# One region that keeps every engine's instructions in the order in which a planner emits them

## The chip, the cores and the metric

The kernel runs on one core of a Trainium2 chip. The metric is the device time of one launch in microseconds (us). The engines of a core run side by side, each through a list of instructions of its own: TensorE (PE, matrix products into PSUM banks), VectorE (DVE), ScalarE (ACT), GpSimd (POOL) and SyncE (SP, which here only starts DMA transfers). An engine takes its list in order, and an instruction that needs a result of another engine waits at the head of the list.

## The reference

Three layers, for 4 batches, 8 heads, 768 steps and 48 numbers per head (4 * 768 = 3072 rows of 8 * 48 = 384 numbers):

```python
f = 1.0 / (1.0 + np.exp(-f_logit))
for t in range(S):
    state = f[:, :, t, :, None] * state + np.einsum('bhd,bhe->bhde', k[:, :, t], v[:, :, t])
    y[:, :, t] = np.einsum('bhd,bhde->bhe', q[:, :, t], state)
...
xn = (x - mu) / np.sqrt(var + 1e-06) * g_ln
x = x + np.maximum(xn @ w_ch1, 0.0) @ w_ch2            # 384 -> 1536 -> 384
...
h = np.maximum(x @ w_in, 0.0)                          # 384 -> 1024
for k in range(K):
    conv_out += conv_w[k][None, None, :] * hp[:, k:k + S, :]
return h * (1.0 / (1.0 + np.exp(-conv_out))) @ w_out   # 1024 -> 384
```

## The kernel before

The sequence is cut into 24 chunks of 128 rows, and three chunks make a unit (8 units). Every chunk goes through gated attention, a LayerNorm and a first MLP (in the code `c1` and `c2`), and every unit through the second layer (`h2`, three taps along the rows, a gate, and the product `o` with the output weights).

**Attention.** DVE makes scans `e` (L471) and `w` (L473) of the forget gates, multiplies q and k by them (L477, L479, L481, L483), PE forms scores in the tile `sc__144` (L497), DVE masks them into `am` (L502), ACT and DVE split them in a high and a low half `as` (L316, L618). ACT also copies transposed keys `kts` out of PSUM, for the state update (PE L529).

**LayerNorm.** DVE L640 and L641 make mean and variance, POOL (L649) turns the variance into the factor `rs`, DVE L653 makes `xn`, and ACT and DVE (L657) split it into two halves `xs`, which a DMA transposes to `xnT`.

**Weights.** They arrive as 64-bit floats in three rotating buffers `raw` and are turned into 32-bit ones on DVE by three instructions, L374, L377 and L380, with the tile `tw` between them. `w__0` and `w__1` are the two buffers of the result. From there ACT and PE (L407, L408) or ACT and DVE (L421) make two half-precision parts.

**Second layer.** For each of the 8 slices of 128 columns PE makes `h2` (L795 to L797), ACT copies it with ReLU to `hr` and multiplies it by the middle tap into `cv`, DVE adds the other two taps (L812, L817). After two slices ACT takes the tanh, DVE multiplies (L827), ACT makes the high half of `g` and DVE the low half (L832). PE then makes `o` (L846 to L848), ACT copies it to the one buffer `ob`, and a DMA takes it out.

**What sets the order.** All this work is written down as jobs of the class `Plan`, each with an engine, a duration that the kernel assumes, a due time, the jobs it needs, and the buffers that it takes and frees. `Plan.run` lists them in Python: again and again it takes, among the jobs that could start next on their engine, the one that is due first, and emits its instructions.

```python
                first = min(c)[0]
                pick = min((k, t, z) for t, k, z in c if t <= first + 0.1)
...
            j = ready[e].pop(z)
            ...
            j.fn()
            j.at = t
            free[e] = t + j.dur
```

So the emission order is the planner's. Before the change it isn't the order on the engines: the framework has a scheduler of its own, which takes the emitted instructions and picks an order for each engine again. The few instructions behind `P.run()` judge whether the inputs lie in the range for which this path is exact (the tile `vr`, one small product on PE at L942); a general path behind a branch is not taken.

Of the kernel before, what the change touches and what calls it, by code (L numbers as in the profile page):

```python
# [205 lines left out]
def fast_path(  # L206
# [7 lines left out]
    P = Plan()  # L214
# [695 lines left out]
    for i, w_ in enumerate((w1s, w2s, wis, wos)):  # L910
        h_ = w_[:, 0].rearrange("p a b -> p (a b)")
        n = h_.shape[1] // 6
        for z in range(6):
            norm2(lambda h_=h_, z=z, n=n: h_[:, z * n:(z + 1) * n], n, 1.0, nrm[:, i, z:z + 1],
                  500.0 + z, [J["late"]])
    P.run()

    n = NACC + NT + NT * NP
    cmp_ = const.tile([128, n], F32, name="cmp")
# [211 lines left out]
@with_exitstack  # L1131
def tile_gated_linear_attention__then__ln_mlp__then__conv_glu(
    ctx: ExitStack, tc: tile.TileContext, q, k, f, v, vd, qk_, f_, gln, w1, w2, wi, cw, wo, out
):
    nc = tc.nc
    vpool = ctx.enter_context(tc.tile_pool(name="verdict", bufs=1))
    bad = vpool.tile([1, 1], I32, name="bad")
    fast_path(tc, v, qk_, f_, gln, w1, w2, wi, cw, wo, out, bad)
    r = nc.values_load(bad, min_val=0, max_val=1)
    with tc.If(r > 0):  # L1140
        pairs = [a.rearrange("b (p j) d s -> (b p) j d s", j=2) for a in (q, k, f, vd)]
        general_path(tc, *pairs, gln, w1, w2, wi, cw, wo, out)
# [44 lines left out]
```

## Time and profile before

| | |
|---|---|
| time, median of 3 runs | 644.81 us (642.97 to 645.51) |
| time of the profiled execution | 643.46 us |
| its span, first to last instruction | 641.4 us |
| busy PE / DVE / ACT / POOL | 586.1 / 501.0 / 386.2 / 42.1 us |
| busy share of the span | 91% / 78% / 60% / 7% |
| chain that ended last | PE 53%, DVE 27%, ACT 8%, DMA 4%, issue 4%, POOL 2% |

The time of the profiled execution is 2.06 us more than its span; that part lies outside the instructions. The busy shares are means over stages that differ, and the chain that ended last tells which engine the end of the kernel went through.

### The profile page before, as it was taken

Reading aid. Unit: us, or ns where it says so; the run is one execution under the profiler, and the core shown is the slowest. Engines: PE = TensorE matmul, PEld = TensorE weight load, DVE = VectorE, ACT = ScalarE, POOL = GpSimd, SP = SyncE. Lnnn points to the kernel's source line nnn. Section 1 sums busy time; section 2 is a strip of 40 time slices with the busy share of each in tenths; the row PEclk is TensorE's granted clock in tenths of the full one; section 3 lists DMA queues with packets and bytes.
Section 4 is the critical chain, followed back from the end, with each engine's and each line's share of the span. In section 5 each row is a group of like instructions: output and inputs, shape, how many; then the busy total and the mean of one; then the engine's idle time right before and its main releaser. Section 6 shows DMA issues by size and latency. Waiting matters only on the chain.

```text
span 641.4 us, 11836 instructions
## 1 busy us (share of the span) xinstructions
PE 586.1 (91%) x4680; PEld 392.7 (61%) x4680; DVE 501.0 (78%) x801; ACT 386.2 (60%) x798; POOL 42.1 (7%) x102
## 2 busy tenths in 40 slices
PE   1869898999798999999989999999989999999993
PEld 1758586767465666666656666666646666665551
DVE  6999989999999898976898787787895773326681
ACT  5888767779896575643675573554563662316471
POOL 3010110010101100010001000010000000000000
PEclk9979999999979899999989999999989999999998
DMA  8757567623224212541521203433221002001001
GB/s 255 184 168 186 175 141 181 189 55 75 68 58 123 63 41 48 143 77 28 103 54 54 80 20 75 118 78 58 46 42 50 14 13 51 25 1 38 25 13 42
DMA packets 75262, 52.24 MB, mean 81 GB/s; under 512 B 51904, under 2 KB 67264, under 8 KB 75200
## 3 DMA queue, kind: packets, MB, share of 16 engines
q1 hardware_dynamic: 75200, 51.42, 31.9%
q8 instruction: 38, 0.62, 0.4%
q14 instruction: 24, 0.20, 0.1%
HBM read 34.63 MB, written 4.72 MB: 61 GB/s over the span
## 4 chain that ended last, share of the span: by engine, by line
PE 53%; DVE 27%; ACT 8%; DMA 4%; issue 4%; POOL 2%; SPq 0%; DVEq 0%; ACTq 0%
PE B L675 5%; PE B L676 5%; PE B L677 5%; PE B L744 5%; PE B L746 5%; PE B L745 5%; PE B L848 4%; PE B L846 4%; PE B L847 4%; PE B L795 2%; PE B L796 2%; PE B L797 2%; DVE tw L377 2%; DVE cv L812 2%; DVE cv L827 2%
## 5 line engine op out<-in xcount | busy, mean ns | idle before, releaser
L675 PE MATMUL B<-xnT,w1s 128*128 128x128 f16 (+1 forms) x432 | 109.2, 275 | 3.0 <-DMA xnT<-xs 3.0
L677 PE MATMUL B<-xnT,w1s 128*128 128x128 f16 (+1 forms) x432 | 109.0, 275 | 0.3 <-ACT w1s L316 0.3
L676 PE MATMUL B<-xnT,w1s 128*128 128x128 f16 (+1 forms) x432 | 109.2, 275 | 0.0
L744 PE MATMUL B<-w2s,hh 128*128 128x384 f16 x288 | 94.5, 329 | 3.1 <-ACT w2s L316 2.1
L746 PE MATMUL B<-w2s,hh 128*128 128x384 f16 x288 | 94.7, 329 | 1.0 <-DVE hh L681 1.0
L745 PE MATMUL B<-w2s,hh 128*128 128x384 f16 x288 | 94.7, 329 | 0.9 <-DVE w2s L421 0.7
L681 DVE SCALAR_TENSOR_TENSOR hh<-B,hh 128x384 f16<-128x384 f32 (+1 forms) x90 | 51.4, 578 | 35.5 <-ACT hh L316 35.1
L795 PE MATMUL B<-x2T,wis 128*128 128x385 f16 x192 | 64.0, 334 | 5.9 <-ACT hr L316 5.9
L846 PE MATMUL B<-wos,g 128*128 128x384 f16 x192 | 63.7, 332 | 3.6 <-ACT g L316 3.6
L848 PE MATMUL B<-wos,g 128*128 128x384 f16 x192 | 63.3, 331 | 2.5 <-DVE g L832 2.4
L796 PE MATMUL B<-x2T,wis 128*128 128x385 f16 x192 | 64.1, 334 | 0.0
L797 PE MATMUL B<-x2T,wis 128*128 128x385 f16 x192 | 64.1, 334 | 0.0
L316 ACT ACTIVATE hh<-B 128x384 f16<-128x384 f32 (+1 forms) x90 | 44.5, 504 | 32.2 <-PE B L677 32.0
L847 PE MATMUL B<-wos,g 128*128 128x384 f16 x192 | 63.4, 330 | 0.0
L676 PEld LDWEIGHTS <-w1s 128*128 128x128 f16 x432 | 42.6, 99 | 16.8 <-issue 4.2
L675 PEld LDWEIGHTS <-w1s 128*128 128x128 f16 x432 | 43.3, 100 | 14.0 <-issue 0.7
L677 PEld LDWEIGHTS <-w1s 128*128 128x128 f16 x432 | 42.6, 99 | 14.9 <-issue 0.5
L812 DVE SCALAR_TENSOR_TENSOR cv<-hr,cws,cv 128x383 f32<-128x383 f32 (+1 forms) x64 | 38.8, 611 | 14.3 <-ACT cv L316 13.8
L497 PE MATMUL sc__144<-qk 64*128 64x128 f32 x384 | 29.6, 292 | 13.9 <-DVE qk L483 13.9
L746 PEld LDWEIGHTS <-hh 128*128 128x128 f16 x288 | 28.3, 98 | 21.8 <-issue 2.1
L744 PEld LDWEIGHTS <-hh 128*128 128x128 f16 x288 | 28.8, 100 | 20.6 <-issue 2.4
L316 ACT ACTIVATE cv<-hr,cws 128x384 f32<-128x384 f32 x64 | 38.7, 610 | 2.5 <-DVE g L832 1.3
(154 smaller groups left out, 1208.8 us busy)
## 6 DMA issues: line engine op xcount, KB each, us to landing
qk<-in_qk__dram SPq DMA_DIRECT2D x48, 192.0 KB, 3.5
raw<-in_w_dram SPq DMA_DIRECT2D x12, 768.0 KB, 5.4
vv<-in_v_dram SPq DMA_DIRECT2D x24, 192.0 KB, 2.5
fb<-in_f__dram SPq DMA_DIRECT2D x48, 96.0 KB, 2.7
out_dram<-ob SPq DMA_DIRECT2D x24, 192.0 KB, 1.9
raw<-in_wi_dram SPq DMA_DIRECT2D x6, 512.0 KB, 4.1
raw<-in_wo_dram SPq DMA_DIRECT2D x4, 768.0 KB, 4.3
xnT<-xs SPq DMA_TRANSPOSE x24, 2.5
```

The costliest lines, as they stand in the source:

```text
L316: nc.scalar.activation(out=out(), in_=in_(), func=func, **{a: z() if callable(z) else z for a, z in kw.items()},)
L675: nc.tensor.matmul(o, w1s[:, 0, kc, ms], x0, start=(kc == 0), stop=False)
L676: nc.tensor.matmul(o, w1s[:, 0, kc, ms], x1, start=False, stop=False)
L677: nc.tensor.matmul(o, w1s[:, 1, kc, ms], x0, start=False, stop=(kc == KC - 1))
L744: nc.tensor.matmul(o(), h[:, 0], w2s[:, 0, m, :], start=(m == 0), stop=False)
L745: nc.tensor.matmul(o(), h[:, 0], w2s[:, 1, m, :], start=False, stop=False)
L746: nc.tensor.matmul(o(), h[:, 1], w2s[:, 0, m, :], start=False, stop=(m == M1 - 1))
L796: nc.tensor.matmul(o, wis[:, 0, kc, ms], r1, start=False, stop=False)
L797: nc.tensor.matmul(o, wis[:, 1, kc, ms], r0, start=False, stop=(kc == KC - 1))
L846: nc.tensor.matmul(p, g[:, 0, ts_], wos[:, 0, m, :], start=(m == 0), stop=False)
L847: nc.tensor.matmul(p, g[:, 0, ts_], wos[:, 1, m, :], start=False, stop=False)
L848: nc.tensor.matmul(p, g[:, 1, ts_], wos[:, 0, m, :], start=False, stop=(m == M2 - 1))
```

## The change

`Plan.run` is called inside a region of the framework. In the region every engine issues its instructions in the order in which they were emitted. The instructions ahead of it and behind it stay outside, and the scheduler places those.

```diff
-    P.run()
+    with tc.manual_schedule():
+        P.run()
```

All lines behind it are one higher in the changed kernel, and the numbers behind some tile names (`cv`, `hr`, `g`, `ob`) are two higher. The number of instructions on each engine stays the same but for a few register and branch instructions. What moves is their order, on all engines. Three places follow.

The first is VectorE in the head of the kernel, where the last of the six pieces of the first weight matrix (`w1`) are turned into 32-bit floats beside the LayerNorm of the second chunk. Before:

```order
L640 BN_STATS st_130<-x_125 128x6
L473 SCALAR_TENSOR_TENSOR w_113<-w_113,d_84 128x516
L374 TENSOR_SCALAR tw_154<-raw_151 128x768
L641 BN_AGGR mvs<-st_130 128x2
L479 TENSOR_TENSOR qk_70<-qk_70,w_113 128x512
L377 SCALAR_TENSOR_TENSOR tw_154<-raw_151,tw_154 128x768
L653 TENSOR_SCALAR xn_123<-x_125,mvs,rs_132 128x384
L380 SCALAR_TENSOR_TENSOR w__1_156<-raw_151,tw_154 128x768
L481 TENSOR_TENSOR w_113<-w_113,e_111 128x4x128
```

And in the changed kernel, on the same engine and in the same part of the program:

```order
L374 TENSOR_SCALAR tw_154<-raw_152 128x768
L377 SCALAR_TENSOR_TENSOR tw_154<-raw_152,tw_154 128x768
L380 SCALAR_TENSOR_TENSOR w__0_155<-raw_152,tw_154 128x768
L374 TENSOR_SCALAR tw_154<-raw_153 128x768
L377 SCALAR_TENSOR_TENSOR tw_154<-raw_153,tw_154 128x768
L380 SCALAR_TENSOR_TENSOR w__1_156<-raw_153,tw_154 128x768
L681 SCALAR_TENSOR_TENSOR hh_137<-B_145,hh_137 128x4x128
L640 BN_STATS st_130<-x_125 128x6
L641 BN_AGGR mvs<-st_130 128x2
L471 SCALAR_TENSOR_TENSOR e_111<-e_111,d_83 128x516
L681 SCALAR_TENSOR_TENSOR hh_138<-B_149,hh_138 128x4x128
L653 TENSOR_SCALAR xn_123<-x_125,mvs,rs_132 128x384
```

The weight pieces stand ahead of the second LayerNorm and of the third chunk's scans (`e_111`), the three instructions of a piece follow each other with nothing between them, and L653 has a scan and an `hh` between itself and L641.

The second place is ScalarE at about a third of the kernel, where it serves one chunk's attention and another unit's MLP (`hh`). `as_122` is the high half of the masked scores of one chunk, and it needs `am_121` of VectorE; `kts_118` is the copy out of PSUM that the state update on PE waits for. Before:

```order
L316 ACTIVATE hh_137<-B_147 128x384
L316 ACTIVATE w_113<-w_113 128x516
L316 ACTIVATE xs_134<-xn_123 128x384
L316 ACTIVATE hh_137<-B_145 128x384
L316 ACTIVATE as_122<-am_121 128x1024
L316 ACTIVATE kts_118<-B_148 128x512
```

And now, on the same engine:

```order
L316 ACTIVATE xs_134<-xn_123 128x384
L316 ACTIVATE hh_137<-B_147 128x384
L316 ACTIVATE hh_137<-B_145 128x384
L316 ACTIVATE kts_118<-B_148 128x512
L316 ACTIVATE as_122<-am_121 128x1024
L316 ACTIVATE hh_138<-B_146 128x384
```

`kts_118` and `as_122` have changed places.

The third place is VectorE at the middle of the kernel, in a unit's second layer. The second gate product of the unit is the L827 that reads `cv_1536` before and `cv_1538` now. Before:

```order
L832 TENSOR_TENSOR g_0_1538<-cv_1535,g_0_1538 128x768
L587 TENSOR_TENSOR sb_95<-B_147,kts_118 48x4x48
L618 TENSOR_TENSOR as_122<-am_121,as_122 128x1024
L812 SCALAR_TENSOR_TENSOR cv_1536<-hr_1534,cws,cv_1536 128x383
L587 TENSOR_TENSOR sb_95<-B_147,kts_118 48x4x48
L817 SCALAR_TENSOR_TENSOR cv_1536<-hr_1534,cws,cv_1536 128x384
L681 SCALAR_TENSOR_TENSOR hh_137<-B_150,hh_137 128x384
L812 SCALAR_TENSOR_TENSOR cv_1535<-hr_1533,cws,cv_1535 128x383
L827 SCALAR_TENSOR_TENSOR cv_1536<-cv_1536,hr_1534 128x768
```

And now:

```order
L832 TENSOR_TENSOR g_0_1540<-cv_1537,g_0_1540 128x768
L812 SCALAR_TENSOR_TENSOR cv_1538<-hr_1536,cws,cv_1538 128x383
L817 SCALAR_TENSOR_TENSOR cv_1538<-hr_1536,cws,cv_1538 128x384
L761 SCALAR_TENSOR_TENSOR x2s_141<-x_0_140,x2s_141 128x384
L502 SCALAR_TENSOR_TENSOR am_121<-sc__144,mask 128x1024
L827 SCALAR_TENSOR_TENSOR cv_1538<-cv_1538,hr_1536 128x768
L812 SCALAR_TENSOR_TENSOR cv_1537<-hr_1535,cws,cv_1537 128x383
L817 SCALAR_TENSOR_TENSOR cv_1537<-hr_1535,cws,cv_1537 128x384
L618 TENSOR_TENSOR as_122<-am_121,as_122 128x1024
L832 TENSOR_TENSOR g_0_1542<-cv_1538,g_0_1542 128x768
```

The attention's instructions L618 and L587 and an `hh` stood ahead of the second gate product and now stand behind it; L761 and L502, which stood ahead of the first gate product or just behind it, now stand between the taps and the second product; and the two tap instructions of a slice are neighbours.

## Rows read from the trace of the kernel before

**Rows 1.** The windows view: busy time of each engine in each stretch.

```profile
core 0: us, PE busy (x) PEld busy (x) DVE busy (x) ACT busy (x) POOL busy (x), PEclk, DMA share, GB/s
40.00:80.00 40.00, 37.04 (x398) 30.13 (x397) 38.73 (x55) 32.80 (x69) 3.90 (x4) 0.96 0.62 185
160.00:200.00 40.00, 35.41 (x290) 23.44 (x290) 38.01 (x61) 34.10 (x78) 3.70 (x6) 0.91 0.29 76
200.00:240.00 40.00, 37.26 (x256) 23.08 (x256) 36.51 (x61) 25.82 (x54) 3.70 (x8) 0.96 0.26 65
240.00:280.00 40.00, 40.00 (x331) 26.00 (x330) 32.51 (x51) 21.92 (x45) 1.88 (x5) 1.00 0.37 87
320.00:360.00 40.00, 37.13 (x283) 23.59 (x282) 33.93 (x54) 24.06 (x45) 3.38 (x6) 0.96 0.23 62
```

**Rows 2.** PE's waits: line, releaser: us in total, times, longest.

```profile
PE sc__144 L497 <- DVE qk L483: 13.9, 3, 13.3
PE B L795 <- ACT hr L316: 5.9, 2, 3.0
PE B L407 <- DVE w__1_156 L380: 5.6, 1, 5.6
PE B L529 <- ACT kts L316: 3.7, 2, 2.7
```

**Rows 3.** DVE's waits between 7 and 209 us, first row, same columns.

```profile
DVE xn L653 <- POOL rs L649: 5.8, 10, 0.7
```

**Rows 4.** Timeline, DVE near 35 us: start, duration, instruction, idle before it.

```profile
34.80 0.17 DVE L641 BATCH_NORM_AGGREGATE mvs<-st 128x2 f32<-128x6 f32 x1
...
36.86 0.48 DVE L653 TENSOR_SCALAR xn<-x,mvs,rs 128x384 f32<-128x384 f32 x1 [0.45 <-POOL rs L649]
```

**Rows 5.** Timeline, DVE near the end: two taps and what follows each.

```profile
583.44 0.62 DVE L812 SCALAR_TENSOR_TENSOR cv<-hr,cws,cv 128x383 f32<-128x383 f32 x1 [3.13 <-ACT cv L316]
583.97 0.55 DVE L756 SCALAR_TENSOR_TENSOR x<-B,x 128x384 f32<-128x384 f32 x1
...
587.84 0.62 DVE L812 SCALAR_TENSOR_TENSOR cv<-hr,cws,cv 128x383 f32<-128x383 f32 x1
588.49 0.62 DVE L817 SCALAR_TENSOR_TENSOR cv<-hr,cws,cv 128x384 f32<-128x384 f32 x1
```

**Rows 6.** Timelines of SP and DVE at the start.

```profile
1.72 1.36 SPq L433 DMA_DIRECT2D fb<-in_f__dram  x2
...
7.14 1.23 DVE L471 TENSOR_TENSOR_SCAN e<-e,d 128x516 f32<-128x516 f32 x1 [4.11 <-ACT e L316]
```

**Rows 7.** Timelines of ACT and PE about 209 us.

```profile
207.63 1.06 ACT L316 ACTIVATE as<-am 128x1024 f16<-128x1024 f32 x1 [2.29 <-DVE am L502]
...
209.23 1.02 PE L529 MATMUL B<-vv,kts 128*112 128x96 f32 x8 [2.75 <-ACT kts L316]
```

**Rows 8.** Timelines of DVE and ACT about 330 us.

```profile
323.78 0.35 DVE L587 TENSOR_TENSOR sb<-B,kts 48x192 f32<-48x192 f32 x1
324.12 1.22 DVE L618 TENSOR_TENSOR as<-am,as 128x1024 f16<-128x1024 f32 x1
325.26 0.61 DVE L812 SCALAR_TENSOR_TENSOR cv<-hr,cws,cv 128x383 f32<-128x383 f32 x1
...
327.95 0.95 DVE L827 SCALAR_TENSOR_TENSOR cv<-cv,hr 128x768 f32<-128x768 f32 x1
...
328.93 0.84 ACT L316 ACTIVATE g<-cv 128x768 f16<-128x768 f32 x1 [0.76 <-DVE cv L827]
329.68 0.47 ACT L316 ACTIVATE hr<-B 128x385 f32<-128x385 f32 x1
```

**Rows 9.** Timelines of ACT and DVE in the last unit.

```profile
610.19 0.49 ACT L316 ACTIVATE ob<-B 128x384 f32<-128x384 f32 x1 [2.92 <-DMA out_dram<-ob]
...
611.74 0.62 DVE L812 SCALAR_TENSOR_TENSOR cv<-hr,cws,cv 128x384 f32<-128x384 f32 x1 [7.01 <-ACT cv L316]
...
627.52 0.96 DVE L832 TENSOR_TENSOR g<-cv,g 128x768 f16<-128x768 f32 x1 [0.91 <-ACT g L316]
```

## The prediction

> **What bounds the kernel now.** I read the windows first [rows 1], because the shares of the whole span hide that two engines take turns. Up to 200 us VectorE is the engine without air: 38.73 us busy of 40 between 40 and 80, 38.01 of 40 between 160 and 200, while PE has 37.04 and 35.41. From 240 us on it is the other way round: PE shows 40.00 of 40, DVE 32.51. Between 200 and 240 both are near it (37.26 and 36.51). So an order that saves or costs VectorE time counts in full up to about 209 us, and behind that only where PE waits for it.
>
> The waits of PE [rows 2] name those places: 13.3 us for the first scores in the head, 5.6 us for a converted weight, 2.7 us (the longer of two) for `kts` on ACT, and twice about 2.9 us (5.9 in all) for `hr` in the second layer. Every such wait has a second price. The granted clock is 0.96 in the windows with a wait of about 3 us and 1.00 between 240 and 280, where PE does not wait [rows 1]; 0.04 of 40 us is 1.6 us of PE time. That is the lower of its two levels (1.2 GHz instead of 2.4) for about 3.2 us behind each wait, and I count 1.6 us for a wait of 3 us that falls away in the part where PE is the bound.
>
> **The change, part by part.** No work is added or removed, so all terms are waits and spacings.
>
> *Neighbours on VectorE: a cost.* The scheduler of before puts other work between an instruction and the one that reads its result; the planner emits them side by side (first place of the change). The trace has both cases. A tap L812 is followed 0.53 us after its start by a stranger (583.44 to 583.97), and 0.65 us after its start by the L817 that reads what it wrote (587.84 to 588.49) [rows 5]. So a dependent pair costs 0.12 us; I take the tap's for all, since taps make the most of them. I counted such pairs in both orders: 109 before, 197 now. Of those, 10 stood in the first 300 or so instructions (up to about 208 us), and 62 stand there now. 52 more times 0.12 is **+6.3 us** where VectorE is the bound, and 36 more behind it (+4.3 us), which PE covers except in the last unit.
>
> [...]
>
> *The wait for POOL: a gain.* L653 needs the factor that POOL makes from L641's variance. Up to 209 us VectorE waits 10 times for it, 5.8 us in all [rows 3], since the old order puts only one or two short instructions between L641 and L653. In the planner's order the stretch between them is longer (first place of the change: a scan, 1.23 us long in rows 6, and an `hh`). Before, at that place, L653 starts 2.06 us after L641 and has waited 0.45 of them [rows 4]: 2.06 us of work between would have been enough, and at the other nine less. I went through all ten places with the durations of what stands between now: 1.3 us or more in each, so I take **-5.8 us**; the bounds are 0 and -5.8.
>
> *The head.* SP now starts the first `fb` ahead of `gl` and `vv`, so 0.9 us sooner than at 1.72, and `fb` is what the first scan at 7.14 waits for through ACT [rows 6]. The two weight instructions that stood ahead of the last step to the first scores now stand behind it, but VectorE still does them before it is free, and ACT now makes the diagonal matrices between the scans' inputs, so VectorE waits for the second scan. I take **-0.5 us**, between 0 and -0.9. The six `w1` pieces come 4 to 6 us sooner and the third chunk's attention some 9 us later; PE's 5.6 us wait for `w__1` goes, but as long as VectorE is the bound PE waits the same sum elsewhere, so this is no term.
>
> *209 us.* Before, ACT takes `as` ahead of `kts`, waits 2.29 us for `am`, and so PE waits 2.75 us for `kts` [rows 7]. Now `kts` stands ahead of `as` (second place). `kts` needs only PE's transpose, long done, so the wait goes; the PE work behind it (`hh` products) is ready, and nothing on PE needs this `as` for about 7 us. **-2.75 and -1.6 of clock: -4.35 us.** Its bounds are -4.35 and 0 (a wait for later VectorE work in its place).
>
> *330 and 470 us.* These two are alike. PE waits for a bank that `hr` frees at 329.68, `hr` stands on ACT behind `g` at 328.93, which waited for the gate product of VectorE at 327.95 [rows 8]. In the third place L618 (1.14 us to the next start) and two L587 (0.34 each) leave the way to that product [rows 8], and so does an `hh`: 1.8 us and the `hh`; the taps in pairs and the tanh wait, now uncovered, put back something like half. So I take half of 2.9 + 1.6 for each, **-2.2 us twice, -4.5 us**; bounds 0 and -9.
>
> *The last unit.* In the old order ACT's copy to `ob` at 610.19 waits 2.92 us for an output transfer, and VectorE idles 7.01 us to 611.74 for a `cv` behind it [rows 9]. The planner puts the first `hr` and `cv` ahead of that copy, so two taps come at about 608.3, but the next `hr` stands behind it as before. Against that, taps of one slice follow each other and the gate product stands directly behind them, so each of four products waits for its tanh, about 0.9 us, with less work of another slice between; and the verdict's five small instructions, outside the region and so free to be moved, stand on VectorE between the gate products and the last low half of unit 6, behind a PE product, about 1.2 us. By hand I come to the last L832 (627.52 before) between 2 us sooner and 4 us later; I take **+2 us**.
>
> Sum: 6.3 - 5.8 - 0.5 = 0 up to 209 us; then 0 - 4.35 - 4.5 + 2 = -6.85 us. The profiled execution took 643.46, so 636.6; it lies 1.35 under the median of the three runs, so on that basis 638.0. **Forecast 638 us.**
>
> **The rivals.** What a measurement can tell from no change here is about 0.5%, 3.2 us.
>
> *More gain, about 630 us.* Neighbours don't cost what I charge, or both waits for `hr` go wholly. The first takes 6.3 us off, the second 4.5 more: 631.7 or 633.5, both 627. For it: the `hr` chain loses that foreign work. Against it: the spacing of the taps [rows 5] for the pairs, and the tanh for the rest.
>
> [...]
>
> *No change, about 645 us.* VectorE stays the bound past 209 us: with 36.51 us of 40 busy until 240 [rows 1] PE only trades the wait for `kts` for one on later scores, and the `hr` chains are as long as they were. Then 0 + 0 + 0 + 2: 645.5 in the profile's terms, 646.8 by the median, and half the `hr` term would put it at 644.6.
>
> *Slower, about 650 us.* The pairs on VectorE cost 6.3 us and the wait for POOL does not go, because POOL's result is late for another reason than its place (in rows 4 it came 2 us behind L641, though two instructions stood between). Then VectorE reaches 209 us 5.8 us later, PE behind it too, and it stays the bound at the next places, so that their terms fall away: 643.46 + 5.8 + 1.35 = 650.6. It decides from the point where less than about 2.6 of the 5.8 us come back.
>
> That the region does nothing can't be: the orders differ on all engines.
>
> **How the numbers follow.** My forecast has 0.38, more gain 0.20, no change 0.22, slower 0.20. Faster by over 0.5% (under 641.6) is the first two: 0.58; within 0.5%: 0.22; slower (over 648.0): 0.20. The range leaves a tenth at each end, so it reaches to 628 (the larger gain without its last 1 us) and to 650 (most of the slower case). The forecast's own range is 633 to 641.
>
> **What would show it.** Pairs: the spacing L812 to L817 is 0.65 in nearly all 32 pairs, and VectorE's busy time and spacing up to 209 us grow. POOL: VectorE's wait for `rs` falls from 5.8 us to under 1 before 209 us. The head: the first scores before 13 us. 209 us: no wait of PE for `kts` over 1 us, and granted clock 1.00 from 210 to 240. 330 and 470: waits for `hr` under 1.5 us each. The end: VectorE's wait of 7 us gone, tanh waits of 0.9 us in its place. The forecast is wrong if PE's waits up to 209 us sum to more than before, if new waits of 3 us appear where PE had 40.00 of 40, or if the last unit takes more than 4 us longer, since nothing covers it.

## The result, and the profile after

The changed kernel takes **651.22 us** (median of 4 runs, 649.53 to 651.42) where the kernel before, run beside it, takes 644.96 (642.97 to 645.51): a ratio of **1.0097**, 95% interval 1.0070 to 1.0124. It is 1% slower. The forecast of 638 us was wrong in sign, and its range missed the time by 1.2 us.

The span is 649.2 us, so 7.8 more than before. The windows of the changed kernel, to be read against [rows 1]:

```profile
core 0: us, PE busy (x) PEld busy (x) DVE busy (x) ACT busy (x) POOL busy (x), PEclk, DMA share, GB/s
40.00:80.00 40.00, 30.38 (x324) 25.43 (x324) 36.37 (x52) 33.05 (x73) 3.44 (x6) 0.91 0.54 170
160.00:200.00 40.00, 32.85 (x259) 22.66 (x260) 38.99 (x61) 36.26 (x77) 4.83 (x8) 0.87 0.22 55
200.00:240.00 40.00, 40.00 (x320) 26.78 (x318) 39.35 (x65) 28.05 (x59) 3.59 (x7) 1.00 0.29 80
320.00:360.00 40.00, 39.56 (x324) 25.96 (x322) 37.86 (x59) 27.62 (x53) 2.62 (x4) 1.00 0.27 72
600.00:650.00 50.00, 33.73 (x172) 17.52 (x171) 20.57 (x33) 19.18 (x32) 0.00 (x0) 0.87 0.07 26
```

The middle has become what was forecast: from 200 to 240 and from 320 to 360 us PE is busy at the full clock. In the two windows ahead of it PE does less than before, and behind 600 us the granted clock is 0.87. PE's waits over the span [rows 2]:

```profile
PE sc__144 L497 <- DVE qk L483: 14.5, 5, 7.1
PE sc__144 L497 <- DMA qk<-in_qk__dram: 13.7, 1, 13.7
PE B L846 <- ACT g L316: 6.6, 3, 3.1
...
PE B L529 <- ACT kts L316: 2.0, 2, 1.3
...
PE B L795 <- ACT hr L316: 0.2, 1, 0.2
```

`hr` is down from 5.9 to 0.2 us, and `kts` from 3.7 to 2.0. But scores (L497) now wait 14.5 us for VectorE besides the first one, up to 7.1 at a time, and `g` 6.6.

Where the time goes is easiest to see in how late PE is. PE makes as many products of each kind in both kernels, and those of one kind come in the same sequence, so I took the n-th one's start in both timelines and subtracted. Positive is later than before; "end" is the difference of the spans, and the columns are named by the time in the kernel before:

| kernel | 219 us | 308 | 359 | 499 | 594 | end |
|---|---|---|---|---|---|---|
| changed kernel | +4.2 | +5.0 | +1.1 | -2.0 | -2.0 | +7.8 |

(In the head it is at +0.4 for the first scores, +4 at 24 us, +8 at 150 and +9.2 at 192.) So there are three parts: a loss up to 200 us, of which 5 us come back at the 209 us place; a gain of 3.9 and 3.1 us at 330 and 470; and a loss of 9.8 us behind 594 us, where the changed kernel was 2.0 us *ahead*.

### The profile page after: what moved, and what is told of

Read it like the earlier page. It is cut to its first block, busy times and chain, and to the rows that moved or that the text cites. A ratio compares the mean times of both kernels' runs of the same rounds, so it can differ in the third digit from the quotient of the medians.

```text
span 649.2 us, 11773 instructions
## 1 busy us (share of the span) xinstructions
PE 589.0 (91%) x4680; PEld 396.4 (61%) x4680; DVE 511.0 (79%) x801; ACT 394.0 (61%) x798; POOL 46.9 (7%) x102
## 4 chain that ended last, share of the span: by engine, by line
PE 52%; DVE 35%; ACT 5%; issue 3%; DMA 2%; POOL 1%; SPq 1%; DVEq 0%; ACTq 0%
PE B L675 5%; PE B L677 4%; PE B L676 4%; PE B L744 4%; PE B L745 4%; PE B L746 4%; PE B L848 4%; PE B L846 4%; PE B L847 4%; DVE cv L812 4%; DVE cv L817 3%; PE sc__144 L497 3%; DVE hh L681 2%; DVE cv L827 2%; DVE g L832 2%
## 5 line engine op out<-in xcount | busy, mean ns | idle before, releaser
L681 DVE SCALAR_TENSOR_TENSOR hh<-B,hh 128x384 f16<-128x384 f32 (+1 forms) x90 | 51.6, 578 | 36.5 <-ACT hh L316 36.3
L846 PE MATMUL B<-wos,g 128*128 128x384 f16 x192 | 65.2, 339 | 6.6 <-ACT g L316 6.6
L848 PE MATMUL B<-wos,g 128*128 128x384 f16 x192 | 65.0, 339 | 2.1 <-DVE g L832 2.1
L847 PE MATMUL B<-wos,g 128*128 128x384 f16 x192 | 64.9, 338 | 0.0
L795 PE MATMUL B<-x2T,wis 128*128 128x385 f16 x192 | 62.9, 328 | 1.5 <-DVE sb L587 1.3
L797 PE MATMUL B<-x2T,wis 128*128 128x385 f16 x192 | 62.9, 327 | 0.0
L796 PE MATMUL B<-x2T,wis 128*128 128x385 f16 x192 | 62.9, 327 | 0.0
L497 PE MATMUL sc__144<-qk 64*128 64x128 f32 x384 | 31.7, 311 | 28.2 <-DVE qk L483 14.5
L675 PEld LDWEIGHTS <-w1s 128*128 128x128 f16 x432 | 43.1, 100 | 13.8
L812 DVE SCALAR_TENSOR_TENSOR cv<-hr,cws,cv 128x383 f32<-128x383 f32 (+1 forms) x64 | 39.1, 611 | 13.7 <-ACT cv L316 13.1
L497 PEld LDWEIGHTS sc__144<-qk 64*128 64x128 f32 x384 | 26.7, 211 | 35.3 <-DVE qk L483 29.6
L316 ACT ACTIVATE cv<-cv 128x768 f32<-128x768 f32 x32 | 26.9, 841 | 27.9 <-DVE cv L817 27.5
L817 DVE SCALAR_TENSOR_TENSOR cv<-hr,cws,cv 128x384 f32<-128x384 f32 (+1 forms) x64 | 39.6, 619 | 2.3
```

Of the source, the lines that this page charges most:

```text
L316: nc.scalar.activation(out=out(), in_=in_(), func=func, **{a: z() if callable(z) else z for a, z in kw.items()},)
L497: nc.tensor.matmul(P("sc", t)[:, j * NP + p, :], k_()[r, p, :], q_()[r, p, :], start=True, stop=True,)
L675: nc.tensor.matmul(o, w1s[:, 0, kc, ms], x0, start=(kc == 0), stop=False)
L812: nc.vector.scalar_tensor_tensor(out=v_[:, y:], in0=hr()[:, z, 0:n - y], scalar=cws[:, m, 0:1], in1=v_[:, y:], op0=ALU.mult, op1=ALU.add,)
L846: nc.tensor.matmul(p, g[:, 0, ts_], wos[:, 0, m, :], start=(m == 0), stop=False)
L847: nc.tensor.matmul(p, g[:, 0, ts_], wos[:, 1, m, :], start=False, stop=False)
```

## The experiments

The same columns stand below for all twelve kernels. They come from two kinds of edit. The region can be entered and left by the planner's clock (its 205 us are about 215 on the chip, its 562 about 582):

```diff
             t, e, z = best
+            now = max(now, t)
+            want = any(lo <= now < hi for lo, hi in spans)
+            if want and inside is None:
+                inside = region()
+                inside.__enter__()
+            elif not want and inside is not None:
+                inside.__exit__(None, None, None)
+                inside = None
...
-    P.run()
+    P.run(tc.manual_schedule, [(205.0, 562.0)])
```

(The edit is against the kernel before; the two numbers are those of mid_only.)

And the planner's numbers can be changed, which changes the order that it emits, and with it the one that the scheduler makes outside the region. Outside the region, and with the numbers as they were, the orders are those of before or of the changed kernel, but for a few rows at the seams. In the five kernels that have the other number from the start (lat_quarter is the first of them), PE takes some `h2` products around 219 us up to 33 us earlier; their first column is read just behind that, at 224 us.

**mid_only.** 

> The region covers only the jobs that the planner starts between 205 and 562 us of its own clock (about 215 to 582 us on the chip); ahead of it and behind it the scheduler orders. Theory A, three separate effects: the loss lies in the head (+4 at 219 us) and in the last two units (+10), and the middle by its order saves PE's two waits for hr, -3.9 and -3.1: 645.0 - 7 = 638, no PE wait over 1 us for hr near 330 and 470. Rival B, slack bought by lateness: the two waits vanished only because PE came 5 us late to them; then the waits return and the time is 644 to 645.

**no_tail**: spans `[(0.0, 562.0)]`. 

> The region ends at 562 us of the planner's clock (about 582 on the chip), so the last two units' second layer is ordered by the scheduler. Theory A: after was 2.0 us ahead of before at 594 us and 7.8 behind at the end, so the last units cost 9.8 and this kernel takes 651.2 - 9.8 = 641.4; VectorE's taps interleave again, no PE wait of 3 us for g. Rival C, the end is late for a reason outside the order there (clock, transfers): 648 to 651.

**tail_only**: spans `[(562.0, 1e9)]`. 

> The region begins at 562 us of the planner's clock; all ahead is ordered by the scheduler as before. Theory A: 645.0 + 9.8 = 654.8, with two PE waits of 3 us for g and the clock below 0.9 behind 600 us. Rival C: 645 to 648.

**head_only**: spans `[(0.0, 205.0)]`. 

> The region ends at 205 us of the planner's clock (about 215 on the chip). Theory A: only the head's loss, 4.2 us at 219 us, of which the middle's two waits (2.9 each) may soak up a part under rival B. A: 645.0 + 4.2 = 649.2. B: the late PE meets no wait for hr, so 645 to 646.

| kernel | us, median | ratio to before (95%) | 219 us | 308 | 359 | 499 | 594 | end |
|---|---|---|---|---|---|---|---|---|
| mid_only | 637.3 | 0.9890 (0.9864 to 0.9916) | +0.1 | +0.1 | -3.7 | -7.2 | -7.2 | -7.2 |
| no_tail | 643.15 | 0.9980 (0.9959 to 1.0000) | +7.6 | +8.9 | +5.1 | +1.9 | +1.9 | +2.3 |
| tail_only | 653.67 | 1.0135 (1.0096 to 1.0174) | +2.2 | +2.1 | +2.3 | +2.4 | +2.4 | +10.9 |
| head_only | 647.59 | 1.0051 (1.0024 to 1.0078) | +6.7 | +6.7 | +5.7 | +5.8 | +5.8 | +5.8 |

Three came out by theory A: 637.3 for 638, 643.15 for 641.4, 653.67 for 654.8. The fourth, 647.59, lies midway between theory A's 649.2 and rival B's 646 and decides nothing. Rival B falls by mid_only, and C by no_tail and tail_only. The middle's gain is its order's: with PE on time (+0.1) both waits for `hr` are gone in mid_only, whose waits of PE between 215 and 582 us are these alone (L806 is the changed kernel's L795):

```profile
PE B L806 <- DVE sb L598: 1.3, 2, 0.9
```

Lateness does buy something, but 1.0 us (head_only between 308 and 359), not 5. The loss of the last units is the order's too: no_tail, with the scheduler there, loses 0.4 behind 594 us, the changed kernel 9.8, tail_only 8.5.

**lat_quarter.** One number of the planner, over the whole region:

```diff
-    LAT = {"PE": 0.25, "DVE": 0.1, "ACT": 0.1, "POOL": 0.15, "SP": 2.5, None: 0.0}
+    LAT = {"PE": 0.25, "DVE": 0.25, "ACT": 0.1, "POOL": 0.15, "SP": 2.5, None: 0.0}
```

The counts of neighbouring pairs in this and the next two expectations leave out the buffer numbers of `cv`, `hr` and `g` and come out higher than the prediction's: 218 in the changed kernel, where that has 197. 

> The changed kernel with one number of the planner other: it takes a VectorE result as usable 0.25 us behind its producer (0.1 in the changed kernel), so it looks for other work between an instruction and its reader. Neighbouring dependent pairs by one count: 218 in the changed kernel, 130 here; in the first 300 instructions 70 and 28 (before: 20); in the last units taps of the next slice stand again between a slice's taps and its gate product. Theory D, pairs and uncovered waits on VectorE make the loss: about 5 us less up to 219 us and about 5 less in the last units, 641. Rival E, what costs is that any order not the scheduler's meets waits it didn't plan for (other engines too): 648 to 653.

**vector_only**: the region with `engines={mybir.EngineType.DVE}`. 

> The region over the whole, but it orders VectorE alone; the other engines are the scheduler's. VectorE's order is that of the changed kernel (70 pairs in the first 300). Theory D: the loss is there in full, about +4 at 219 us and +8 to +10 in the last units, 649 to 652. Rival E: the loss belongs to the other engines, 641 to 645.

**all_but_vector**: the region with the other four engines. 

> The region orders all engines but VectorE, whose order is the scheduler's: 26 pairs in the first 300, but in the last units, where ScalarE's order leaves no choice, the changed kernel's row of two taps and a gate product. Theory D: the head's loss goes to 0 to 2 us at 219, the last units keep theirs, so 645 to 648. Rival E: +4 or more at 219, 650 to 653.

| kernel | us, median | ratio to before (95%) | 219 us | 308 | 359 | 499 | 594 | end |
|---|---|---|---|---|---|---|---|---|
| lat_quarter | 639.35 | 0.9919 (0.9888 to 0.9950) | -0.3 | -0.1 | -4.2 | -8.4 | -8.4 | -4.8 |
| vector_only | 658.44 | 1.0220 (1.0176 to 1.0265) | +5.7 | +12.3 | +10.3 | +8.3 | +8.3 | +13.8 |
| all_but_vector | 668.24 | 1.0346 (1.0307 to 1.0386) | +16.3 | +20.8 | +18.5 | +16.5 | +16.5 | +26.3 |

lat_quarter came as theory D had it: 12 us less than the changed kernel by one number. The other two missed. I had taken it that the loss sits in one engine's order; instead the two half-kept orders are the slowest kernels of all. all_but_vector has few pairs, and VectorE waits more than in any other kernel. From its waits between 7 and 225 us:

```profile
DVE xn L653 <- POOL rs L649: 6.2, 9, 0.9
...
DVE st L640 <- ACT x L316: 4.6, 1, 4.6
DVE tw L374 <- DMA raw<-in_wo_dram: 3.1, 1, 3.1
DVE w__0_155 L380 <- PE B L407: 2.7, 1, 2.7
```

So pairs are one price on VectorE, and waits at the head of its list are another, and the second can be larger. To part them I went through VectorE's timeline: for each instruction the time to the next start, less the wait that the waits view lists ahead of the next one (it leaves out those under 0.15 us), is its spacing; what it has over the lower quartile of the same instruction's spacings in the two kernels I call drag. Up to the point where VectorE has done the same work (187.7 us of it, at 204.8 us before):

| kernel | there at | drag | waits |
|---|---|---|---|
| before | 204.8 us | 3.8 to 4.2 | 14.5 |
| changed kernel | 213.5 | 11.1 | 15.7 |
| head_only | 216.1 | 11.4 | 18.0 |
| lat_quarter | 210.5 | 5.8 | 17.9 |

lat_quarter has 42 pairs fewer in the first 300 instructions than the changed kernel, and 5.3 us less drag: 0.13 us for each. Not all drag is pairs: by the same working all_but_vector, with 26 pairs where the kernel before has 20, has about 7 us, some 2 us more than 0.13 us for each pair would give. lat_quarter has *more* waits, and among them one stands out, 5.9 us for `craw`, the convolution's weights, which VectorE decoded ahead of the first scores.

**tail_lat**: the changed kernel up to 562 us of the planner's clock, then the number of lat_quarter.

```diff
-            end = t + j.dur + j.lat
+            end = t + j.dur + j.lat + (0.15 if e == "DVE" and t > 562.0 else 0.0)
```

> The changed kernel, and only behind 562 us of the planner's clock the planner takes a VectorE result as usable 0.25 us behind its producer. VectorE's order is the changed kernel's up to the last 36 rows or so; there, taps of the next slice stand between a slice's taps and its gate product in most cases, while the count of neighbouring pairs stays (218 to 216) and the verdict stays in the last unit but one. Theory F, the gate product directly behind its taps makes most of the 9.8 us of the last units: 651.2 - 5 = 646, waits of VectorE for the tanh behind 600 us from 4.5 to under 2, no PE wait of 3 us for g. Rival G, the pairs or the verdict make it: 650 to 652.

**lat_craw**: lat_quarter, and the planner's number for the arrival of `craw`.

```diff
     cj = P.job("SP", 0.45, 20.0, lambda: nc.sync.dma_start(
-        out=craw.rearrange("p n t -> p (n t)"), in_=cw.bitcast(I32)))
+        out=craw.rearrange("p n t -> p (n t)"), in_=cw.bitcast(I32)), lat=24.0)
```

> lat_quarter, and the planner is told that the convolution's weights (craw) land 24 us after their transfer is started, so that VectorE does not decode them ahead of the first scores (it waited 5.9 us for them there). Theory H, VectorE is the bound up to 209 us, and a wait at the head of its list comes back in full or nearly: 634 to 636. Rival I, the wait is made good before 219 us, where PE stood only 0.3 us ahead of the kernel before: 638 to 640.

**lat_craw_no_tail**: lat_craw with the spans `[(0.0, 562.0)]`. 

> lat_craw with the region ending at 562 us of the planner's clock, so that the scheduler orders the last units. The last units cost 4.3 us against the kernel before in lat_quarter and 0.5 with the scheduler, so 4 us less than lat_craw: 630 to 632 under theory H, 635 under rival I.

**lat_mid**: lat_quarter with the spans `[(205.0, 562.0)]`. 

> The region only from 205 to 562 us of the planner's clock, with the 0.25 us of lat_quarter. The middle gained 8.1 us there between 219 and 594 us, head and end are the scheduler's: 644 - 8 + 0.5 = 636.5, as in mid_only (637.3) or 1 us less. If the middle's gain needs the planner's head, 640 to 644.

**head_lat**: lat_craw with the spans `[(0.0, 205.0)]`. 

> head_only (the region over the first 205 us of the planner's clock, the scheduler behind it) with the two numbers of lat_craw: 0.25 us behind a VectorE result, and craw known to land late. Neighbouring pairs in the first 300 VectorE instructions 31 instead of 70. Theory D, it is this order's pairs and the waits at the head of VectorE's list that cost, not keeping an order as such: head_only's 6.7 us behind at 219 us becomes 4 ahead, so head_only's 647.6 becomes 638 to 641 (the waits for hr at 330 and 470 are back, since the scheduler orders there). Rival E, any order kept in the head costs: 646 to 649.

| kernel | us, median | ratio to before (95%) | 219 us | 308 | 359 | 499 | 594 | end |
|---|---|---|---|---|---|---|---|---|
| tail_lat | 644.3 | 0.9998 (0.9981 to 1.0014) | +2.3 | +3.3 | -0.5 | -3.7 | -3.7 | -1.9 |
| lat_craw | 632.1 | 0.9798 (0.9782 to 0.9815) | -4.5 | -4.5 | -8.6 | -12.8 | -12.8 | -11.0 |
| lat_craw_no_tail | 629.57 | 0.9776 (0.9745 to 0.9806) | -5.4 | -5.4 | -9.5 | -13.7 | -13.7 | -13.9 |
| lat_mid | 634.49 | 0.9849 (0.9814 to 0.9885) | -1.5 | -1.5 | -5.6 | -9.8 | -9.8 | -9.8 |
| head_lat | 642.04 | 0.9950 (0.9928 to 0.9971) | -4.7 | -0.6 | -0.9 | -1.3 | -1.3 | -1.0 |

tail_lat, which moves rows of VectorE and ScalarE there, settles the last units: as many pairs, but 1.8 us lost behind 594 us where the changed kernel loses 9.8. Theory F holds, and of rival G the pairs fall. Of the verdict this kernel says less, since its five instructions, though still in the last unit but one, now stand behind that unit's last L832 (601.31 behind 600.43) and not ahead of it; that it costs nothing is read from the changed kernel's own rows below. VectorE's waits behind 600 us in tail_lat have none for L827 left (4.5 us in five waits in the changed kernel):

```profile
DVE cv L812 <- ACT cv L316: 5.9, 2, 5.7
DVE g L832 <- ACT g L316: 2.7, 3, 0.9
```

and its window behind 600 us has the clock at 0.93, as the kernel before has there:

```profile
600.00:650.00 50.00, 28.08 (x167) 15.81 (x167) 18.25 (x30) 18.02 (x31) 0.00 (x0) 0.93 0.07 26
```

lat_craw (632.1, 634 to 636 expected) agrees with theory H and not with I: 4.2 us come back at 219 us, and 7 in the medians, of the 5.9 us at the head of VectorE's list. It isn't that wait alone, since the number moves the order on VectorE and ScalarE in many places up to 270 us: at equal work VectorE's waits are 4.0 us less than in lat_quarter and its drag 0.3 more. lat_mid's expected 636.5 lies within its interval (632.7 to 637.3); of the 2 us that it is better, 1.5 are there at 219 us, where the scheduler had another emission order to start from.

In head_lat the loss of head_only turns from +6.7 to -4.7 at 219 us, as expected, so rival E falls. Then 4.1 us of it are lost again ahead of 308 us, where the scheduler orders, and the time is 1 us above what I gave it. PE's waits between 225 and 275 us, none in the kernel before, account for it together with the granted clock of 0.91 from 240 to 260 us: 2.2 us, and 0.09 of 20 us is 1.8 (L638 is the changed kernel's L627, which needs the halves `as`):

```profile
PE B L638 <- DVE as L629: 1.5, 1, 1.5
PE B L638 <- ACT as L327: 0.7, 1, 0.7
```

The waits for `hr`, which its expectation brought back, are not there; waits for `g` stand in their place. **lat_craw_no_tail has the lowest median, 629.57 us, 2.2% under the kernel before**: the whole region but for the last units. Its runs (628.71 to 632.55) overlap those of lat_craw (631.06 to 632.47), so that these two differ is not shown. The last units cost 1.8 us in lat_craw, and 3.6 in lat_quarter, not the 4.3 of the expectation.

## Why the prediction was wrong

**Pairs: right.** 6.3 us were charged up to 209 us for 52 pairs; the drag on VectorE grew by 7.3 (3.8 to 11.1). The 1.0 us between need not be pairs, as all_but_vector shows. The spacing is where it was, in the changed kernel's last units:

```profile
593.63 0.62 DVE L812 SCALAR_TENSOR_TENSOR cv<-hr,cws,cv 128x383 f32<-128x383 f32 x1
594.28 0.62 DVE L817 SCALAR_TENSOR_TENSOR cv<-hr,cws,cv 128x384 f32<-128x384 f32 x1
```

0.65 us, as in [rows 5]. The Trainium skill ("VectorE: DVE Perf Modes", "The DRAIN you can't avoid") says that the next instruction does not start until the pipe has emptied, and that one which is not held starts earlier. The rows agree: the L817 that reads L812's result starts 0.65 us behind it, when its 0.62 us are over, and the stranger of [rows 5] 0.53 us behind it, ahead of that. That it is the reading which holds L817 back, this case's rows tell and that section doesn't: L817 starts 0.62 to 0.66 us behind its L812 in all 64 pairs of the changed kernel, and another instruction starts 0.51 to 0.54 us behind an L812 in 31 of 33 cases of the kernel before. 42 pairs fewer in lat_quarter took 5.3 us of drag with them.

**The wait for POOL, and the sum "= 0 up to 209 us": the step that failed first.** The prediction took off the waits of the old order, 5.8 us for POOL, and charged the new order none. VectorE's waits between 7 and 209 us in the changed kernel, to be set beside [rows 3] and the 4.11 us of [rows 6]:

```profile
DVE gl L867 <- DMA gl<-in_gln_dram: 4.9, 1, 4.9
DVE xn L653 <- POOL rs L649: 2.2, 5, 0.5
DVE xs L657 <- ACT xs L316: 1.9, 1, 1.9
DVE am L502 <- PE sc__144 L497: 1.8, 4, 0.8
DVE kts L542 <- PE B L529: 1.6, 1, 1.6
DVE hh L681 <- ACT hh L316: 0.9, 2, 0.7
DVE w L473 <- ACT w L316: 0.8, 1, 0.8
```

POOL fell by 3.6, not 5.8, and five waits that the old order hardly had put 7.0 us in its place (`xs`, `am`, `kts`, `hh`, `w`). Other waits of the old order, 3.1 us, went: for `x2s` (2.1), `x` and `raw`.

The first microseconds show how an instruction at the head of VectorE's list holds all behind it. SP starts `fb` at 1.50 now, 0.2 us sooner and not 0.9, and `gl` third and not first. L867, which needs `gl`, stands ahead of the first scan and waits for it until 7.41, so that the scan begins at 7.49 where it began at 7.14, though ACT's `e`, its input, is there at 6.36: a loss where I had -0.5.

Waits in all 14.5 before and 15.7 after, so +1.2 where the prediction had -6.3; the three other kernels with this order in the head have 13.9, 18.0 and 20.0. VectorE was 8.7 us late at equal work, PE 9.2 us at 192, where the sum had 0. At 219 us the kernel is 8.5 us behind the forecast (+4.2 for -4.35), more than half of the 14.6 us by which it is at the end (+7.8 for -6.85).

**209 us: right.** PE has no wait for `kts` there, its lateness falls from 9.2 at 192 us to 4.2 at 219 (forecast -4.35), and the clock is 1.00 from 200 to 240. What the prediction's rival said did happen, but ahead of that place: at 184 us PE waits 7.13 us for scores.

```profile
184.29 2.08 PE L497 MATMUL sc__144<-qk 64*128 64x128 f32 x16 [7.13 <-DVE qk L483]
```

**330 and 470 us: right, and larger.** -3.9 and -3.1 for -2.2 each; mid_only has them without the head and the end, -3.8 and -3.5.

**The last unit, "+2": the other step that failed.** It is +9.8, so 7.8 us more, by these rows of VectorE, PE and ACT in the changed kernel:

```profile
600.56 0.62 DVE L817 SCALAR_TENSOR_TENSOR cv<-hr,cws,cv 128x384 f32<-128x384 f32 x1
602.09 0.96 DVE L827 SCALAR_TENSOR_TENSOR cv<-cv,hr 128x768 f32<-128x768 f32 x1 [0.91 <-ACT cv L316]
...
603.96 0.96 DVE L832 TENSOR_TENSOR g<-cv,g 128x768 f16<-128x768 f32 x1 [0.23 <-ACT g L316]
...
614.06 0.62 DVE L812 SCALAR_TENSOR_TENSOR cv<-hr,cws,cv 128x384 f32<-128x384 f32 x1 [7.80 <-ACT cv L316]
...
633.73 0.96 DVE L832 TENSOR_TENSOR g<-cv,g 128x768 f16<-128x768 f32 x1 [0.91 <-ACT g L316]
```

```profile
603.98 0.34 PE L846 MATMUL B<-wos,g 128*128 128x384 f16 x1 [2.98 <-ACT g L316]
...
633.76 0.50 PE L846 MATMUL B<-wos,g 128*128 128x384 f16 x1 [3.10 <-ACT g L316]
```

```profile
612.89 0.49 ACT L316 ACTIVATE hr<-B 128x385 f32<-128x385 f32 x1 [2.92 <-PE B L797]
```

The gate product stands directly behind its last tap and waits 0.91 us for the tanh, six times behind 590 us. I had charged this to the last unit alone, and there it is what I had, four times 0.9: from the tap behind the long wait to the last L832 19.7 us (614.06 to 633.73) where it was 15.8 (611.74 to 627.52 in [rows 9]), +3.9. But the unit ahead of it pays the same: its last L832 comes 12.0 us behind the end of PE's `h2` (591.95) and came 8.4 behind it (593.98 to 602.43), +3.6. Both make PE wait 3 us for `g`, and behind each wait the granted clock is at its lower level, which it is not in the kernel before from 603 to 609 and from 627 to 633 us (1.00):

```profile
606.00:609.00 3.00, 3.00 (x11) 1.49 (x10) 0.26 (x1) 0.33 (x1) 0.00 (x0) 0.50 0.18 66
634.00:640.00 6.00, 5.83 (x19) 2.54 (x18) 0.69 (x1) 0.49 (x1) 0.00 (x0) 0.50 0.11 38
```

The 28 products of `o` behind the last L832 of a unit take 6.4 and 7.3 us where they took 4.7, and the end comes 15.5 us behind the last L832 and not 13.9: +1.7 and +1.6. Against that stands the gain for the copy to `ob`, where I hoped for 3.4: `hr` at 612.89 now waits for the late PE, and what is left between the two units, taken as a remainder, is 0.9. 3.9 + 3.6 + 1.7 + 1.6 - 0.9 = 9.9. The prediction had put the unit ahead of the last one and the clock behind PE's waits at nothing. The verdict, charged 1.2, costs nothing: its five instructions end at 603.7, and L832 waits 0.23 us more for ACT's `g`, which ends at 603.92.

**The slower rival**, 650.6, had the number by luck, for half the reason. VectorE was late by the pairs, but POOL's wait did mostly go, the middle kept its gains, and it was the last units that brought the sum to +7.8: 4.2 at 219 us, -6.2 to 594, +9.8.

## What to carry to other kernels

An order that is kept must be charged for its own waits, not only relieved of the old order's: walk the list of the engine that is the bound and ask of each instruction what it needs and whether that is there, and do it first where nothing covers the end of the kernel. A planner whose latencies are too short emits a reader right behind its producer; giving it 0.25 us in place of 0.1, and for one transfer 24 us (in lat_quarter it took 7.8, where the planner had 2.5), moved this kernel from 1% slower to 2% faster than the scheduler's order. Keep an order on all engines of a stretch or on none, as far as the two half-kept orders here tell, and measure stretch by stretch: here the middle gained, and the head and the end lost.

## What was not expected of the hardware

The same order doesn't cost the same each time in the head. The changed kernel, no_tail, tail_lat and head_only have the same order on all engines up to about 215 us, and PE stands at +4.2, +7.6, +2.3 and +6.7 us at 219; with the scheduler's order there, mid_only and tail_only stand at +0.1 and +2.2. One profile of this kernel tells a loss in the head to some 2 or 3 us only. What differs is VectorE's waits and not its spacing: by the working above its drag is about 11 us in all four, and its waits are 15.7, 20.0, 13.9 and 18.0. The largest part is L681's waits for ScalarE's `hh`, 0.9, 4.9, 0 and 2.5 us. Why ScalarE was later there was not found.

A wait of 3 us of PE at the end cost, beside the wait itself, 1.7 and 2.6 us in the products behind it (4.7 us became 6.4 and 7.3 for 28 of them), at a granted clock of 0.50 from 606 to 609 and from 634 to 640 us. tail_only has the same two waits (2.98 and 3.10 us) and 0.50 behind them; tail_lat, where the longest wait of PE behind 600 us is 1.1 us, has 1.00 from 600 to 631.5.
